# Where to fetch 22 streamed weight granules: spread over the whole segment, or over its q, k, v projections alone

## The chip, the cores and the metric

The kernel runs on one core of a Trainium2 chip. The metric is the device time of one execution in microseconds (us), as the median of several runs. The word "clock" means the mean granted TensorE clock as a share of full speed.

## The reference, cut to what matters

The work is a layer norm, a recurrent attention with memory (A), and a small expert part at the end (B). Part A is nearly all of the time:

```python
mem = mem0                                        # 8 rows
for s in range(64):                               # 64 segments of 32 rows, width 1024
    h = concatenate([mem, x[s]])                  # 40 rows
    q, k, v = h @ Wq, h @ Wk, h @ Wv              # each to 32 heads x 128
    p = softmax(where(mask, q @ k.T * scale, -1e9))
    o = (p @ v) @ Wo                              # the output projection
    mem = o[:8]                                   # goes into the next segment
    outs.append(o[8:])
```

The four weight matrices are 8 MB each in bf16, and every segment needs all 32 MB. Neither kernel keeps them all in the core's memory (42 of 64 pieces stay there, as told below), and a segment can't start before the memory rows of the one before are there.

## The kernel before

The weights are cut into 64 **granules** of 512 KB: 48 for q, k, v (six phases of eight), then 16 for the output projection. 42 are resident; 22 are **streamed**, which means that they are fetched again in each segment into a ring of six slots. Half of each of three of them (`HELD`) stays in PSUM and is copied from there by ScalarE.

```python
N_RES = 42
N_SLOT = 6
HELD = (18, 27, 36)
PHASES = [(0, 0), (1, 0), (0, 1), (1, 1), (2, 0), (2, 1)]   # (0 q, 1 k, 2 v; half)
streamed = set(((2 * i + 1) * NG) // (2 * n_str) for i in range(n_str))   # NG = 64, n_str = 22
# = 1 4 7 10 13 16 18 21 24 27 30 33 36 39 42 45 | 48 50 53 56 59 62: six in the projection
```

A slot is given back, and the next granule is issued on SyncE's queue, when the last matmul that reads the slot is over:

```python
def used(g):
    if g in streamed:
        fetch()          # takes a slot of the ring and issues the next granule's DMA
```

In a segment, 32 rows go through every granule as the main pass (24 new rows and 8 memory rows; `PSm`, then `WO` in the projection). The other 8 rows of each segment do not depend on the memory. They are called the **left rows**, and those of four segments are taken together (`PSl`, `WL`). With j = s % 4, the left rows' pass through q is made at j = 2, through k at j = 3, through v at j = 0, and their output projection at j = 3. The end of a segment reads, cut:

```python
for w in range(16):
    Gv = granule(48 + w)
    project(WO, w, Gv, lhs_main, w == 15)
    if j == 3:
        if 48 + w in streamed:
            project(WL, w, Gv, lhs_left, first=not started)   # 6 passes here
        else:
            deferred.append((w, Gv))
    used(48 + w)
OB = ...                                    # copy of WO by ScalarE and VectorE
for w, Gv in deferred[:3]:
    project(WL, w, Gv, lhs_left)            # 3 passes while the copies run
mem_to_st(OB, nxt["st"])                    # transposes of the memory rows: next segment's operand
# the other 7 left passes follow in the next segment's q and k
OL = one.tile([P, 256], BF16, tag="pm", name="OL")   # output of the left rows; PM of softmax has this tag too
```

## Time and profile before

| | before |
|---|---|
| median of 3 runs | 2130.74 us (2130.5 to 2137.17) |
| profiled run | span 2125.5 us, clock 0.954 |
| TensorE busy | 82% |
| DMA | 768.74 MB, 362 GB/s |
| a segment | 30.9 us: j = 0 to 3 take 31.2, 30.7, 30.9, 30.8 |
| of it the projection | 7.3, 8.9, 9.3, 10.6 us |

The segments' times are worked out from TensorE's rows: from the first main pass of one segment to that of the next, means over the segments of one j. One wait, VectorE's for a store (engine, tile, what it waited for, us in total, times, longest):

```profile
DVE PM L497 <- DMA out_dram<-OL: 59.8, 15, 4.6
```

Softmax's PM shares its buffer with OL, so once in four segments it waits until the store of OL has landed.

### The profile page before, as it was taken

The numbers are of one execution on the slowest core, as the hardware profiler recorded it, in microseconds if no ns is written. First come the engines' busy times: TensorE is split into PE (matmuls) and PEld (weight loads), VectorE is DVE, ScalarE is ACT, GpSimd is POOL, SyncE is SP. The second block draws the span as 40 slices with busy tenths as digits, with TensorE's granted clock in tenths as the row PEclk, the third lists the DMA queues.
The fourth block names the chain that finished last, engine by engine and source line by source line (L and its number), as shares of the span: only waits on it lengthen the run. The fifth ranks groups of instructions, "written<-read, shape, count | busy, mean of one in ns | idle before, by whom it ended". The sixth has DMA issues, their size and how long they took to land.

```text
span 2125.5 us, 82723 instructions
## 1 busy us (share of the span) xinstructions
PE 1732.3 (82%) x36202; PEld 883.3 (42%) x36202; DVE 746.4 (35%) x2328; ACT 713.0 (34%) x1738; POOL 540.6 (25%) x1030
## 2 busy tenths in 40 slices
PE   2678888888889888887888888888888888888776
PEld 1234444444444444444444434444444444444341
DVE  5523332333333233333333333333333333333330
ACT  3533333333333333332333333333333323333220
POOL 4422223222222322222232222223222222222110
PEclk8689999999999999999999999999999999999996
DMA  9899999999999999999999999999999999999998
GB/s 357 333 366 389 337 375 361 381 353 364 377 353 369 361 379 347 360 381 356 371 346 389 348 365 365 372 367 347 372 356 383 358 370 363 347 365 351 350 339 341
DMA packets 294351, 768.74 MB, mean 362 GB/s; under 512 B 37458, under 2 KB 42770, under 8 KB 293988
## 3 DMA queue, kind: packets, MB, share of 16 engines
q1 hardware_dynamic: 267652, 732.79, 93.3%
q0 software_dynamic: 23520, 26.06, 3.7%
q8 instruction: 283, 4.64, 0.8%
q10 hardware_dynamic: 2816, 4.59, 0.6%
q14 instruction: 80, 0.66, 0.1%
HBM read 750.68 MB, written 12.59 MB: 359 GB/s over the span
## 4 chain that ended last, share of the span: by engine, by line
DMA 50%; PE 41%; DVE 3%; issue 3%; ACT 3%; POOL 0%; ACTq 0%; DVEq 0%; SPq 0%; POOLq 0%
DMA g<-in_A_Wo_dram 21%; PE PSm L590 21%; DMA g<-in_A_Wv_dram 11%; DMA g<-in_A_Wq_dram 7%; PE PSl L603 6%; PE OA L641 4%; DMA out_dram<-OL 4%; DMA g<-in_A_Wk_dram 2%; PE WL L641 2%; PE PTq L430 2%; DMA wres<-in_A_Wo_dram 1%; DMA g<-in_B_w_up_dram 1%; PE SPS L474 1%; DMA g<-in_B_w_gate_dram 1%; PE PTq L442 1%
## 5 line engine op out<-in xcount | busy, mean ns | idle before, releaser
L590 PE MATMUL PSm<-wres,ST 128*32 128x512 bf16 x8192 | 757.0, 394 | 19.7 <-DVE ST L309 17.9
L590 PE MATMUL PSm<-g,ST 128*32 128x512 bf16 x4096 | 415.8, 395 | 98.4 <-DMA g<-in_A_Wv_dram 53.1
L590 PEld LDWEIGHTS <-ST 128*32 128x32 bf16 x12288 | 294.3, 97 | 429.8 <-issue 198.8
L641 PEld LDWEIGHTS <-OT 128*32 128x32 bf16 x8192 | 215.8, 98 | 170.8 <-issue 156.4
L220 ACT COPY g<-HELD 128x1024 bf16<-128x1024 bf16 x189 | 191.3, 1012 | 204.6 <-PE PSm L590 115.4
L611 ACT CAST XB<-PSm 128x512 bf16<-128x512 f32 x256 | 150.2, 587 | 322.2 <-PE PSm L590 321.6
L641 PE MATMUL OA<-wres,OT 128*32 128x256 bf16 x5120 | 236.1, 280 | 18.8 <-issue 12.7
L641 PE MATMUL OA<-g,OT 128*32 128x256 bf16 x3072 | 160.2, 280 | 95.9 <-DMA g<-in_A_Wo_dram 89.4
L603 PE MATMUL PSl<-wres,STL 128*32 128x512 bf16 x2048 | 199.9, 391 | 14.0 <-DVE XBl L615 13.4
L340 POOL DMA_DIRECT2D QKL<-qkl_d x126 | 92.1, 731 | 264.3 <-issue 118.3
L538 ACT CAST OT<-OA 128x128 bf16<-128x128 f32 x256 | 68.2, 266 | 267.8 <-PE OP L532 266.0
L462 POOL COPY KT<-QKL 128x128 bf16<-128x128 bf16 x128 | 37.8, 295 | 415.9 <-PE OA L641 310.1
L676 POOL DMA_DIRECT2D out_dram<-OB x256 | 129.8, 514 | 52.3 <-DVE OB L672 35.9
L538 DVE CAST OT<-OP 128x128 bf16<-128x128 f32 x128 | 37.3, 292 | 265.1 <-PE OP L532 265.1
L603 PEld LDWEIGHTS <-STL 128*32 128x32 bf16 x3072 | 86.0, 99 | 97.8 <-issue 38.4
L479 DVE TENSOR_REDUCE NM<-SPS 128x8 f32<-128x320 f32 x128 | 62.9, 491 | 158.3 <-PE SPS L474 158.3
L623 ACT CAST VM<-PSm 128x512 bf16<-128x512 f32 x128 | 77.2, 603 | 120.1 <-PE PSm L590 114.9
L603 PE MATMUL PSl<-g,STL 128*32 128x512 bf16 x1024 | 103.0, 392 | 11.5 <-DVE XBl L615 8.7
L430 PE MATMUL PTq<-IDENT,XB 128*128 128x128 bf16 x1024 | 103.7, 225 | 5.5 <-ACT XB L611 5.0
L450 POOL DMA_DIRECT2D qkl_d<-QS x64 | 36.6, 572 | 278.4 <-ACT QS L446 278.4
L430 PEld LDWEIGHTS <-XB 128*128 128x128 bf16 x1024 | 59.3, 99 | 114.6 <-ACT XB L611 60.6
L437 DVE COPY KT<-PTq 128x512 bf16<-128x512 bf16 x128 | 53.4, 417 | 134.8 <-PE PTq L430 134.5
(140 smaller groups left out, 2310.3 us busy)
## 6 DMA issues: line engine op xcount, KB each, us to landing
g<-in_A_Wo_dram SPq DMA_DIRECT2D x384, 512.0 KB, 7.2
g<-in_A_Wq_dram SPq DMA_DIRECT2D x321, 512.0 KB, 7.6
g<-in_A_Wk_dram SPq DMA_DIRECT2D x257, 512.0 KB, 6.5
g<-in_A_Wv_dram SPq DMA_DIRECT2D x257, 512.0 KB, 7.2
g<-in_A_Wq_dram SPq DMA_DIRECT2D x63, 256.0 KB, 5.9
g<-in_A_Wk_dram SPq DMA_DIRECT2D x63, 256.0 KB, 5.5
g<-in_A_Wv_dram SPq DMA_DIRECT2D x63, 256.0 KB, 7.0
qkl_d<-QS POOLq DMA_DIRECT2D x64, 128.0 KB, 6.1
```

Of the source, the lines that this page charges most:

```text
L220: nc.scalar.copy(out=t[:, 1024:2048], in_=held[what[1]][:, :].bitcast(BF16))
L340: nc.gpsimd.dma_start(out=t[:, :, :], in_=qkl_d[s // 4][:, half, :, s % 4, :].rearrange("m p c -> p m c"))
L430: nc.tensor.transpose(out=PTq[:, il, :, :].rearrange("p j r -> p (j r)"), in_=XB[:, il * P:(il + 1) * P], identity=IDENT[:, :])
L437: nc.vector.tensor_copy(out=keys(half)[:, :, 0:32], in_=pv)
L479: nc.vector.tensor_reduce(out=NM[:, :], in_=S8, axis=AX.X, op=ALU.max, negate=True)
L538: copy(out=OT[half][:, 2 * ph + jl, :, :], in_=ov[:, :, 0:SEG])
L590: nc.tensor.matmul(PSm[32 * jq:32 * jq + 32, :], lhsT=ST[:, kc, :], rhs=Gv[:, 512 * jq:512 * (jq + 1)], start=(kc == 0), stop=(kc == KC - ...
L603: nc.tensor.matmul(PSl[32 * jq:32 * jq + 32, :], lhsT=cur["stl"][:, kl, :], rhs=Gl[:, 512 * jq:512 * (jq + 1)], start=(kl == 0), stop=(kl ...
L611: nc.scalar.copy(out=XB[:, :], in_=PSm[:, :])
L623: nc.scalar.copy(out=VM[half][:, :], in_=PSm[:, :])
L641: nc.tensor.matmul(PS[32 * g:32 * g + 32, 0:256], lhsT=lhs(h), rhs=Gv[:, D * hs + 256 * g:D * hs + 256 * (g + 1)], start=(first and hs == ...
L676: nc.gpsimd.dma_start(out=out2[s * SEG:s * SEG + XM, 256 * g:256 * (g + 1)], in_=OB[32 * g:32 * g + XM, 0:256])
```

## The change

It makes the whole output projection resident and spreads the 22 streamed granules over the 48 of q, k, v. The intent is that the projection waits for no transfer, and that the DMA, which ran below its best rate in the middle of q, k, v, gets more to do there. Left rows' passes become filler: at j = 1 and 2 the next segment's left passes of q or k on resident granules are put around the transposes of the memory rows, and at j = 3 all 16 left projection passes are made in the projection and around the transposes. OL moves to another buffer. Cut to its core:

```diff
-HELD = (18, 27, 36)
+HELD = (14, 22, 29)
-    streamed = set(((2 * i + 1) * NG) // (2 * n_str) for i in range(n_str))
+    streamed = set(((2 * i + 1) * 48) // (2 * n_str) for i in range(n_str))
+    # = 1 3 5 7 9 12 14 16 18 20 22 25 27 29 31 33 36 38 40 42 44 46
 ...
-            project(WO, w, Gv, lhs_main, w == 15)
+            project(WO, w, res_tiles[48 + w], lhs_main, w == 15)
+            if j == 3:
+                if w == 2:
+                    XLT = load_left(G, again=True)      # was at w == 8
+                if 5 <= w < 14:
+                    project_left()                      # 9 passes here
 ...
-        for w, Gv in deferred[:3]:
-            project(WL, w, Gv, lhs_left)
+        if j == 3:
+            fill = [project_left] * (16 - n_wl)
+        elif j == 1 or j == 2:
+            for mat in nl:                              # next segment's left passes of q or k
+                begun[mat] = left_bank()
+                fill = [lambda ...: left_pass(L, kc, res_tiles[g])
+                        for kc in range(KC) if 8 * mat + kc not in streamed]
+        for fn in fill[:len(fill) // 2]:
+            fn()
         if s + 1 < NSEG:
             mem_to_st(OB, nxt["st"])
+        for fn in fill[len(fill) // 2:]:
+            fn()
 ...
-                OL = one.tile([P, 256], BF16, tag="pm", name="OL")
+                OL = one.tile([P, 512], BF16, tag="vm", name="OL")
```

More of the change, by code (lines that the diff above doesn't have):

```diff
@@ L72 @@
     n_str = NG - N_RES
-    streamed = set(((2 * i + 1) * NG) // (2 * n_str) for i in range(n_str))
+    streamed = set(((2 * i + 1) * 48) // (2 * n_str) for i in range(n_str))
+    N_LATE = 10
     assert all(g in streamed and g < 48 for g in HELD)
@@ L208, in fetch @@
                 pool = wres
-                if g >= 48:
+                if g >= NG - N_LATE:
                     if late["pool"] is None:
@@ L390, in routed_e, with left_of, left_pass, left_bank @@
         nc.vector.tensor_copy(out=SIG[:, :], in_=PSG[0:2, 0:1])
+    def left_of(s):
+        G, j = divmod(s, 4)
+        if s == 0:
+            return {0: 0, 1: 0, 2: 0}
+        if j == 0:
+            return {2: G}
+        return {j - 2: G + 1} if j >= 2 and G + 1 < NT else {}
+    def left_pass(L, kc, Gv):
+        for jq in range(4):
+            nc.tensor.matmul(L["ps"][32 * jq:32 * jq + 32, :], lhsT=cur["stl"][:, kc, :],
+                             rhs=Gv[:, 512 * jq:512 * (jq + 1)], start=(not L["had"]), stop=(len(L["had"]) == KC - 1),
+                             tile_position=(0, 32 * jq))
+        L["had"].append(kc)
+    def left_bank():
+        return {"ps": psL.tile([P, 512], F32, tag="accl", name="PSl"), "had": []}
+    begun = {}
     for s in range(NSEG):
         G, j = divmod(s, 4)
-        if s == 0:
-            left = {0: 0, 1: 0, 2: 0}
-        elif j == 0:
-            left = {2: G}
-        elif j >= 2 and G + 1 < NT:
-            left = {j - 2: G + 1}
-        else:
-            left = {}
+        left = left_of(s)
         VM = {}
@@ L582 @@
             PSm = psA.tile([P, 512], F32, tag="acc", name="PSm")
-            PSl = psL.tile([P, 512], F32, tag="accl", name="PSl") if mat in left else None
+            L = begun.pop(p, None) or left_bank() if mat in left else None
             lag, behind = 2 if j == 0 else 0, []
@@ L595 @@
                                             op0=ALU.bitwise_or)
-                if PSl is None:
+                if L is None:
                     used(g)
@@ L601 @@
                     kl, Gl = behind.pop(0)
-                    for jq in range(4):
-                        nc.tensor.matmul(PSl[32 * jq:32 * jq + 32, :], lhsT=cur["stl"][:, kl, :],
-                                         rhs=Gl[:, 512 * jq:512 * (jq + 1)], start=(kl == 0), stop=(kl == KC - 1),
-                                         tile_position=(0, 32 * jq))
+                    if kl not in L["had"]:
+                        left_pass(L, kl, Gl)
                     used(8 * p + kl)
@@ L612 @@
                 hooks.setdefault((p + 1, (3, 2, 3, 2)[p]), []).insert(0, lambda m=mat, h=half, b=XB: transposes(m, h, b))
-                if PSl is not None:
+                if L is not None:
                     XBl = two.tile([P, 512], BF16, tag="xb", name="XBl")
-                    (nc.scalar.copy if p == 2 else nc.vector.tensor_copy)(out=XBl[:, :], in_=PSl[:, :])
+                    (nc.scalar.copy if p == 2 else nc.vector.tensor_copy)(out=XBl[:, :], in_=L["ps"][:, :])
                     hooks.setdefault((p + 1, (5, 4, 6, 4)[p]), []).insert(
@@ L619 @@
                 c0 = half * 512
-                if PSl is not None:
-                    nc.scalar.copy(out=VL[:, c0:c0 + 512], in_=PSl[:, :])
+                if L is not None:
+                    nc.scalar.copy(out=VL[:, c0:c0 + 512], in_=L["ps"][:, :])
                 VM[half] = one.tile([P, 512], BF16, tag="vm", name="VM")
@@ L649, in lhs_left, with project_left @@
             return OTL[:, h, :, :].rearrange("p s r -> p (s r)")
-        deferred = []
-        started = False
+        n_wl = 0
+        def project_left(WL=WL if j == 3 else None):
+            nonlocal n_wl
+            project(WL, n_wl, res_tiles[48 + n_wl], lhs_left, first=(n_wl == 0))
+            n_wl += 1
         for w in range(16):
@@ L657 @@
                 attend(1, 1)
-                if j == 3:
+            project(WO, w, res_tiles[48 + w], lhs_main, w == 15)
+            if j == 3:
+                if w == 2:
                     XLT = load_left(G, again=True)
-            Gv = granule(48 + w)
-            project(WO, w, Gv, lhs_main, w == 15)
-            if j == 3:
-                if 48 + w in streamed:
-                    project(WL, w, Gv, lhs_left, first=not started)
-                    started = True
-                else:
-                    deferred.append((w, Gv))
-            used(48 + w)
+                if 5 <= w < 14:
+                    project_left()
         OB = one.tile([P, 512], BF16, tag="vm", name="OB")
@@ L679 @@
         todo = [((0, 2), store)]
-        for w, Gv in deferred[:3]:
-            project(WL, w, Gv, lhs_left)
+        fill = []
+        nl = left_of(s + 1) if s + 1 < NSEG else {}
+        if j == 3:
[3 more added lines that the diff above has]
+                begun[mat] = left_bank()
+                fill = [lambda kc=kc, g=8 * mat + kc, L=begun[mat]: left_pass(L, kc, res_tiles[g])
+                        for kc in range(KC) if 8 * mat + kc not in streamed]
+        for fn in fill[:len(fill) // 2]:
+            fn()
         if s + 1 < NSEG:
             mem_to_st(OB, nxt["st"])
+        for fn in fill[len(fill) // 2:]:
+            fn()
         if j == 3:
-            spots = [(0, 1), (0, 3), (0, 5), (0, 7), (1, 1), (1, 3), (1, 5), (1, 7), (2, 1), (2, 3)]
-            for pk, (w, Gv) in zip(spots, deferred[3:]):
-                todo.append((pk, lambda w=w, Gv=Gv, WL=WL, lhs=lhs_left: project(WL, w, Gv, lhs)))
             def left_norm(G=G, X=XLT):
@@ L693, in left_store @@
                 residual(WL, X[:, 0:256], P, False)
-                OL = one.tile([P, 256], BF16, tag="pm", name="OL")
-                nc.scalar.copy(out=OL[:, :], in_=WL[:, 0:256])
+                OL = one.tile([P, 512], BF16, tag="vm", name="OL")
+                nc.scalar.copy(out=OL[:, 0:256], in_=WL[:, 0:256])
                 o4 = out2[4 * G * SEG:4 * (G + 1) * SEG, :].rearrange("(s r) d -> s r d", s=4)
                 for g in range(4):
-                    nc.gpsimd.dma_start(out=o4[:, XM:SEG, 256 * g:256 * (g + 1)], in_=OL[32 * g:32 * (g + 1), :])
+                    nc.gpsimd.dma_start(out=o4[:, XM:SEG, 256 * g:256 * (g + 1)], in_=OL[32 * g:32 * (g + 1), 0:256])
             todo += [((0, 6), left_norm), ((1, 6), left_store)]
```

## The prediction

> **What bounds the kernel now.** A segment is one round of q, k, v (48 weight granules of 512 KB), attention, and the output projection (16 granules). 42 granules stay in the chip; 22 are fetched again in each of the 64 segments through six slots, three of them by half. I read the page first, then the DMA share and rate by stretch, then who waited for whom, then the instructions at a segment's end.
>
> From the page, the engines' busy time, the DMA total and the chain that ended last:
>
> ```profile
> PE 1732.3 (82%) x36202; PEld 883.3 (42%) x36202; DVE 746.4 (35%) x2328; ACT 713.0 (34%) x1738; POOL 540.6 (25%) x1030
> ...
> DMA packets 294351, 768.74 MB, mean 362 GB/s; under 512 B 37458, under 2 KB 42770, under 8 KB 293988
> ...
> DMA 50%; PE 41%; DVE 3%; issue 3%; ACT 3%; POOL 0%; ACTq 0%; DVEq 0%; SPq 0%; POOLq 0%
> ```
>
> Half of the chain is transfers, 41% is TensorE, so the bound must change hands inside a segment. Stretches of two segments show it (columns: window, length, busy time of PE, PEld, DVE, ACT, POOL, granted clock, DMA share, GB/s):
>
> ```profile
> 1009.20:1013.00 3.80, 3.80 (x69) 1.71 (x69) 0.78 (x4) 1.13 (x2) 2.11 (x5) 1.00 1.02 409
> 1013.00:1019.00 6.00, 6.00 (x102) 2.69 (x98) 1.80 (x4) 3.66 (x5) 0.85 (x2) 1.00 0.98 332
> 1019.00:1026.00 7.00, 6.76 (x162) 3.25 (x154) 3.78 (x11) 2.48 (x5) 1.69 (x4) 1.00 0.98 347
> 1029.40:1039.90 10.50, 6.04 (x166) 4.08 (x165) 1.26 (x7) 1.70 (x8) 1.11 (x3) 1.00 1.04 410
> 1039.90:1053.00 13.10, 13.10 (x240) 6.11 (x244) 4.91 (x14) 5.80 (x8) 3.35 (x8) 1.00 0.97 337
> ```
>
> In the output projection (1029.4 to 1039.9) TensorE works 6.0 of 10.5 us and the DMA runs at 410 GB/s: transfers bind. In the middle of q, k, v TensorE has no gap and the rate is 332 to 347: the slots are full and TensorE binds. The DMA share says 0.97 in both, so I go by the rate. The waits agree (engine, line, waited for, us in total, times, longest):
>
> ```profile
> PE OA L641 <- DMA g<-in_A_Wo_dram: 89.4, 147, 2.5
> PE PSm L590 <- DMA g<-in_A_Wv_dram: 53.1, 81, 2.6
> PE PSm L590 <- DMA g<-in_A_Wq_dram: 23.0, 38, 2.1
> PE PSl L603 <- DVE XBl L615: 22.1, 3, 8.7
> PE PTm L308 <- ACT OB L671: 20.3, 48, 0.4
> PE PSm L590 <- DMA g<-in_A_Wk_dram: 19.6, 32, 2.3
> PE PSm L590 <- DVE ST L309: 17.9, 63, 0.3
> ```
>
> TensorE waits 185 us for streamed weights (89.4 + 53.1 + 23.0 + 19.6), 2.9 us a segment. A segment takes 30.9 us: the copies that end a segment (OB) run from 115.4 to 2063.8, 63 segments. The end of one:
>
> ```profile
> 1007.43 0.40 PE L641 MATMUL OA<-wres,OT 128*32 128x256 bf16 x8
> 1008.26 0.23 PE L308 MATMUL PTm<-IDENT,OB 128*128 128x128 bf16 x1 [0.42 <-ACT OB L671]
> 1008.65 0.23 PE L308 MATMUL PTm<-IDENT,OB 128*128 128x128 bf16 x1 [0.17 <-DVE OB L672]
> 1009.16 0.40 PE L590 MATMUL PSm<-wres,ST 128*32 128x512 bf16 x4 [0.28 <-DVE ST L309]
> 1009.39 0.39 PE L603 MATMUL PSl<-wres,STL 128*32 128x512 bf16 x4
> ```
>
> 0.42 + 0.17 + 0.28 = 0.87 us of idle TensorE around the memory rows' transposes, and 0.22 us from one pass to the next.
>
> **What the Trainium skill says.** Perfetto Trace Analysis, Optimization Strategy: where the most contended engine changes over time, interleaving the regimes may help. The trace has two such regimes; before, the streamed granules are already interleaved with both, and the change separates them. DMA: Bandwidth & Descriptors, "Anatomy of one DMA", gives about 2.0 us fixed cost for a DMA, mostly the receipt (for GpSimd's path). Here granules go through SyncE: the shortest issue-to-landing time of a 512 KB granule in the trace is 3.39 us, for one issued 7.7 us after the granule before it, and 1.3 us of that is data at 410 GB/s, so about 2.1 us fixed: it agrees. The same page, "Where 436 GB/s comes from", sets about 358 GB/s for HBM to SBUF and 435 for the fabric. The trace sustains 410, and 428 in one stretch of 2 us (1054 to 1056), so 358 doesn't bind and I take 415.
>
> **The change, part by part.** Bytes do not change: still 22 granules, three by half, 10.75 MB a segment; with the other traffic (queues 0 and 8, 30.7 MB over 64 segments) 11.23 MB, or 27.1 us at 415 GB/s: 1.32 us a whole granule (11.23 MB over 20.5 granules), 0.66 a half one. Now all 22 sit between granules 1 and 46 of q, k, v.
>
> (a) TensorE's own time. Summing its rows by the segment's place in a group of four (j = 0 to 3) and taking out the DMA waits, I get 29.1, 25.8, 27.3, 29.4 us, mean 27.9. No matmul is added or removed. Filler hides at most 0.87 us in three segments of four, so the mean falls to some 27.5. That can't be had while transfers need 27.1 plus idle time.
>
> (b) The gap without a release. After granule 46 no slot comes free until granule 1 of the next segment is used. From the start of granule 46 to the residual's matmul is 1.14 us (1028.29 to 1029.43). From there to the next segment's first pass, DMA waits taken out, the trace has 6.6 (j = 0), 7.1, 7.1 and 9.6 us. The change moves work into it: for j = 1 four left passes (granules 0, 2, 4, 6; 0.87 us, mostly hidden, so about 6.9 in all, from j = 0's base), for j = 2 five (7.1), for j = 3 all 16 left projection passes instead of 9, 7 more by 0.22, less the hidden waits and some DMA waits not recognised as such: 9.4. In j = 0 the lagging left passes of v add 0.65. Two more passes and the release, 0.7 us, end it. Gap: 6.6 + 0.65 + 1.85 = 9.1, then 8.75, 8.95, 11.25; mean 9.5 us.
>
> (c) What the DMA can do in the gap: refill six slots, 6 x 1.32 = 7.9 us. Then it idles, and it starts again with one granule, number 14, a half one: 3.4 - 0.65 = 2.75 us until it lands.
>
> (d) The cycle from granule 46 to the next granule 46: gap 9.5, restart 2.75, then the other 15 streamed granules, 13 x 1.32 + 2 x 0.66 = 18.5. Sum 30.75 us, against 30.9 before. TensorE needs about 27.5 for it, so it waits for transfers in the second half of q, k, v instead of in the projection.
>
> So the 89 us of Wo waits go, and Wv, Wk and Wq waits grow by about as much. Over 63 segments 0.15 us are 9 us.
>
> (e) Start and end. The first segment loads the same 64 granules; the last ten still need the prologue's memory back. The last segment fills six slots for the expert's weights during the projection, as before. I take 0 for both, with 5 us of doubt.
>
> (f) A side change: the tile OL moves from tag "pm" to "vm". VectorE waited 59.8 us in 15 waits with PM for OL's store to land. That goes, but ScalarE will wait with OL for OB's stores, issued about 12 granules earlier. Both lie in j = 0's q, k, v, where TensorE would now wait for weights anyway: 0 to 1 us each, 10 us in all at most.
>
> Sum: 2130.7 - 9, and a few us for (f): 2120.
>
> **Rivals.** First, smoothing works: six full slots at the start of q, k and no wait in the projection let TensorE run near its own 27.5 us. Half of the way there is 29.2, 107 us less, 2024. For it speak the 89.4 us of Wo waits in the chain and that the starved DMA of q, k, v gets work. Against it: 27.1 us of transfers must then fit with almost no idle time, and the gap makes idle time in each segment. Second, the gap costs more: the restart ramps slowly, and the left passes added to the projection stand where nothing is released. One us more a cycle gives 2183. The 9.4 us of j = 3 speak for it: that cycle alone comes to 32.5. Third, the swap comes out even, as reckoned. A fourth, that the new OL wait stalls ScalarE and thereby the transposes of k, would show in j = 0 only, at 2 to 3 us by 16: up to 40 us.
>
> **Range and chances.** The sum hangs on two small differences, so 0.8 us a segment of doubt, some 50 us, is fair, with more room downward than upward, since an error in the gap or in the restart can go only as far as TensorE's bound. Range 2055 to 2185. Beyond 2% either way needs 43 us, 0.68 us a segment. Faster 0.33, within 2% 0.46, slower 0.21.
>
> **What would show it.** Right: no wait of OA for a Wo granule; waits of PSm for Wv, Wk and Wq together near 200 us; a rate over 400 GB/s in v; in the last 2 us or more of the projection, and longest for j = 3, a rate well under 200; first landings 3 us after granule 1. Wrong: if segments of j = 3 are no longer than others, the gap isn't the cost; if the rate in the projection stays at 400 to its end, the slots were not refilled and (c) falls; if waits for streamed weights fall below 100 us, the first rival holds.

## The result, and the profile after

| | before | after |
|---|---|---|
| median of 4 runs | 2131.62 us | 2386.43 us (2380.71 to 2395.69) |
| profiled run | 2125.5 us, clock 0.954 | 2379.1 us, clock 0.909 |
| segment, j = 0 to 3 | 31.2, 30.7, 30.9, 30.8 us | 33.7, 33.0, 34.8, 37.9 us (mean 34.9) |
| of it the projection | 7.3, 8.9, 9.3, 10.6 us | 6.9, 7.1, 7.6, 10.6 us |

The kernel got slower by 12%: the ratio is 1.1194, with a 95% interval from 1.1148 to 1.1239.

From the page after, the totals and the chain that ended last:

```profile
PE 1834.6 (77%) x36202; PEld 931.2 (39%) x36202; DVE 749.1 (31%) x2328; ACT 714.8 (30%) x1738; POOL 541.7 (23%) x1030
...
DMA packets 245967, 768.74 MB, mean 323 GB/s; under 512 B 37458, under 2 KB 42770, under 8 KB 245604
...
DMA 55%; PE 37%; issue 3%; ACT 2%; DVE 2%; POOL 0%; ACTq 0%; DVEq 0%; SPq 0%; POOLq 0%
```

The same matmuls and the same bytes took longer. TensorE's busy time rose by 102 us with the same number of matmuls. The lower clock accounts for most of it: 1732.3 us at a clock of 0.954 would be 1818 at 0.909, 86 us more (an estimate). The DMA's mean rate fell from 362 to 323 GB/s, and the chain has more of transfers in it.

TensorE's waits after (who waited for what, us in total, times, longest), and one of ScalarE's:

```profile
PE PSm L605 <- DMA g<-in_A_Wv_dram: 176.9, 278, 2.6
PE PSm L605 <- DMA g<-in_A_Wq_dram: 155.1, 164, 3.3
PE PSm L605 <- DMA g<-in_A_Wk_dram: 37.1, 68, 1.8
PE PTm L309 <- ACT OB L685: 7.2, 17, 0.4
```

```profile
ACT XB L624 <- DMA out_dram<-OL: 55.0, 14, 5.2
```

No streamed Wo granule is left to wait for, as intended. But the waits for Wv, Wq and Wk are 369 us (176.9 + 155.1 + 37.1), against 95.7 before and about 200 predicted. The transposes (PTm) wait for OB 17 times, once in each segment with j = 0, instead of 48 times.

The end of a segment with j = 2 and the start of the next, as TensorE ran it (start, length, line, what, count; a wait stands in brackets):

```profile
1026.25 1.93 PE L654 MATMUL OA<-wres,OT 128*32 128x256 bf16 x64
1028.01 0.60 PE L405 MATMUL PSl<-wres,STL 128*32 128x512 bf16 x8
1028.61 0.56 PE L309 MATMUL PTm<-IDENT,OB 128*128 128x128 bf16 x2
1029.09 0.83 PE L405 MATMUL PSl<-wres,STL 128*32 128x512 bf16 x12
1029.75 0.39 PE L605 MATMUL PSm<-wres,ST 128*32 128x512 bf16 x4
...
1036.76 0.40 PE L605 MATMUL PSm<-g,ST 128*32 128x512 bf16 x4 [1.62 <-DMA g<-in_A_Wq_dram]
```

Between the last projection pass and the first main pass no wait is left: the left passes (PSl) do cover the three waits of 0.42, 0.17 and 0.28 us that stood there before. Seven us into the new segment TensorE waits for a weight.

SyncE's issues of granules around that point, and the same time in stretches (window, length, busy time of PE, PEld, DVE, ACT, POOL, clock, DMA share, GB/s):

```profile
1020.40 1.75 SPq L223 DMA_DIRECT2D g<-in_A_Wk_dram  x2
1030.40 0.33 SPq L220 DMA_DIRECT2D g<-in_A_Wk_dram  x1
1030.83 1.48 SPq L223 DMA_DIRECT2D g<-in_A_Wq_dram  x3
1032.93 0.33 SPq L220 DMA_DIRECT2D g<-in_A_Wq_dram  x1
1034.24 1.09 SPq L223 DMA_DIRECT2D g<-in_A_Wk_dram  x2
```

```profile
1018.00:1027.00 9.00, 7.32 (x184) 4.74 (x187) 2.71 (x10) 2.61 (x14) 0.55 (x1) 0.81 1.01 407
1028.00:1031.00 3.00, 2.90 (x51) 1.14 (x41) 0.48 (x2) 0.86 (x2) 2.12 (x5) 1.00 0.10 33
1031.00:1035.00 4.00, 4.00 (x65) 1.71 (x64) 1.57 (x6) 2.02 (x3) 0.84 (x2) 1.00 0.78 197
1035.00:1044.00 9.00, 6.70 (x109) 2.84 (x104) 2.11 (x4) 3.19 (x5) 0.97 (x3) 0.81 1.03 397
```

The last issue before the pause ends at 1022.15; the next comes at 1030.40. The six slots are filled meanwhile, at 407 GB/s, and then the DMA stands still (33 GB/s from 1028 to 1031). That is the gap as predicted. What was not predicted comes next: from 1031 to 1035 four granules have been issued within 2 us, then more, and the rate is only 197 GB/s. In the 9 us after 1035 TensorE works 6.7 us, and the DMA is at 397. The DMA share says 0.78 at 197 GB/s. The Trainium skill, Perfetto Trace Analysis, "Identifying the Most-Contended Engine", says that the occupancy of the 16 DMA engines misleads; this trace agrees.

Averaged over segments, from the first issue after the pause on, the rate in one us after another is 33, 218, 186, 230, 289, 359, 360, 349, 390, and then about 405 for some us. Individual packets of 4096 B mostly take 159 ns. Of those that start 1 to 4 us after the first issue, 28% take 300 ns or more (mean of all 297 ns); at 10 to 14 us it is 1% (mean 164 ns).

### The profile page after: what moved, and what is told of

The parts are those of the page before. It is cut to its first block, busy times and chain, and to the rows that moved or that the text cites. A ratio compares the mean times of both kernels' runs of the same rounds, so it can differ in the third digit from the quotient of the medians.

```text
span 2379.1 us, 82768 instructions
## 1 busy us (share of the span) xinstructions
PE 1834.6 (77%) x36202; PEld 931.2 (39%) x36202; DVE 749.1 (31%) x2328; ACT 714.8 (30%) x1738; POOL 541.7 (23%) x1030
## 4 chain that ended last, share of the span: by engine, by line
DMA 55%; PE 37%; issue 3%; ACT 2%; DVE 2%; POOL 0%; ACTq 0%; DVEq 0%; SPq 0%; POOLq 0%
DMA g<-in_A_Wv_dram 32%; DMA g<-in_A_Wq_dram 18%; PE PSm L605 14%; PE OA L654 11%; PE PSl L405 4%; PE WL L654 3%; PE OA L545 2%; DMA wres<-in_A_Wo_dram 1%; PE PTq L445 1%; DMA g<-in_B_w_up_dram 1%; PE PTm L309 1%; PE OA L547 1%; DMA g<-in_A_Wk_dram 1%; PE OA L303 1%; DMA XP<-in_A_x_dram 1%
## 5 line engine op out<-in xcount | busy, mean ns | idle before, releaser
L605 PE MATMUL PSm<-g,ST 128*32 128x512 bf16 x5632 | 599.7, 413 | 373.4 <-DMA g<-in_A_Wv_dram 176.9
L605 PE MATMUL PSm<-wres,ST 128*32 128x512 bf16 x6656 | 685.4, 410 | 6.0 <-DVE ST L310 5.1
L605 PEld LDWEIGHTS <-ST 128*32 128x32 bf16 x12288 | 325.7, 97 | 803.9 <-issue 588.5
L654 PE MATMUL OA<-wres,OT 128*32 128x256 bf16 x8192 | 325.8, 294 | 41.1 <-issue 29.1
L654 PEld LDWEIGHTS <-OT 128*32 128x32 bf16 x8192 | 229.7, 103 | 70.3 <-issue 52.6
L405 PE MATMUL PSl<-wres,STL 128*32 128x512 bf16 x1664 | 157.5, 393 | 19.2 <-DVE XBl L628 13.4
L405 PE MATMUL PSl<-g,STL 128*32 128x512 bf16 x1408 | 142.9, 390 | 9.0 <-DVE XBl L628 8.7
L545 PEld LDWEIGHTS <-VM 32*128 32x128 bf16 x2048 | 65.2, 93 | 89.7 <-issue 73.6
```

What stands on the lines that cost most here:

```text
L405: nc.tensor.matmul(L["ps"][32 * jq:32 * jq + 32, :], lhsT=cur["stl"][:, kc, :], rhs=Gv[:, 512 * jq:512 * (jq + 1)], start=(not L["had"]), ...
L545: nc.tensor.matmul(o, lhsT=VM[half][q0:q0 + 32, il * P:(il + 1) * P], rhs=PTm[q0:q0 + 32, il, 0:NK], start=True, stop=False, tile_position ...
L605: nc.tensor.matmul(PSm[32 * jq:32 * jq + 32, :], lhsT=ST[:, kc, :], rhs=Gv[:, 512 * jq:512 * (jq + 1)], start=(kc == 0), stop=(kc == KC - ...
L654: nc.tensor.matmul(PS[32 * g:32 * g + 32, 0:256], lhsT=lhs(h), rhs=Gv[:, D * hs + 256 * g:D * hs + 256 * (g + 1)], start=(first and hs == ...
```

## The experiments

The first theory after the result was: the pause of about nine us in the giving back of slots costs the time, because transfers come back slowly after it (**pause theory**). Its rivals were: the filler and the left passes' new places cost it (**filler theory**); the half granule with which transfers restart (**half granule**); TensorE's lower clock (**clock theory**); and, later, that the q, k stage with its main passes slows transfers whatever came before (**stage theory**), or that the queue is short because the slots come free one by one (**supply theory**). Fourteen runs were made (none has the number 7); all results were correct.

### e1_place: the new placement alone

The changed kernel's placement and OL, with the left rows' work as before: no early passes, the left projection 6 + 3 + 7.

```diff
-                if 5 <= w < 14:
-                    project_left()
+                if w in (0, 2, 5, 8, 11, 14):
+                    project_left(w, Gv)
 ...
-        # filler around mem_to_st at j = 1, 2, 3
+        for _ in range(3 if j == 3 else 0):
+            project_left(*pend.pop(0))       # before mem_to_st; the other 7 in the next q, k
```

> The new placement of the streamed granules alone; the left rows' passes and the left projection stand where they stood before (6 of the 16 left projection passes in the projection, 3 ahead of the transposes, 7 in the next q and k; no left pass begun early). Pause theory (no slot comes free during the projection, the transfers stop, and come back slowly): the pause stays, only shorter by about 1.5 us for j = 3 and 0.3 us for j = 1 and 2, so 16 x (1.5 + 0.6) = 34 us off: about 2350, 2310 to 2385. Filler theory (the left passes moved into the projection are what costs): near before, 2100 to 2160.

It took 2357.54 us, ratio 1.1064 (1.1011 to 1.1116), clock 0.913. The placement alone brings nearly all of the loss, so the filler theory falls.

### e2_filler: the new left rows' work alone

The changed kernel with the old placement and HELD; the left passes go around the transposes as in the change, and a left projection pass on a streamed granule stays beside its main pass.

```diff
-HELD = (14, 22, 29)
+HELD = (18, 27, 36)
-    streamed = set(((2 * i + 1) * 48) // (2 * n_str) for i in range(n_str))
+    streamed = set([1, 4, 7, ..., 42, 45, 48, 50, 53, 56, 59, 62])
```

> The filler and the moved left projection alone, with the placement of before (six streamed granules in the projection). Pause theory: slots come free all through the projection, so no stop of the transfers; 2080 to 2145, about 2115, since 0.9 us of idle TensorE around the transposes is used in half of the segments. Filler theory: most of the 250 us stays, above 2250.

It took 2105.37 us, ratio 0.9871 (0.983 to 0.9913), clock 0.952: a little faster than before. With e1_place this settles that the placement is the cost and the rest of the change a small gain.

### e3_mix2, e4_mix4, e11_mix8: two, four, eight of the 22 in the projection

They are e2_filler with other lists, and HELD moved to fit. For e11_mix8 the ten last-loaded resident granules are loaded by a step of their own in the first segment.

```diff
+    streamed = set([1, 3, 6, ..., 44, 46, 52, 60])                      # e3_mix2
+    streamed = set([1, 4, 6, ..., 44, 46, 50, 54, 58, 62])              # e4_mix4
+    streamed = set([1, 5, 8, ..., 42, 46, 49, 51, 53, 55, 57, 59, 61, 63])  # e11_mix8
```

> As the changed kernel, but 2 of the 22 streamed granules in the projection (its granules 4 and 12), 20 in q, k, v. Pause theory: the longest stretch without a release falls from 9 us to about 4, less than the six slots hold, so the transfers never stop: 2060 to 2170, and no stretch of a microsecond under 150 GB/s between segments. Filler theory: above 2250 still.

It took 2231.66 us, ratio 1.0487 (1.0425 to 1.0549). The expectation missed: I had thought that two releases in the projection break the pause and so cure it. Transfers do not stop any more, but the mean rate in the us after the start of a segment is still 230, 133, 239, 242, 251, 285, 318 (none under 150 was expected). On average 1.2 granules are under way in the first of these us and 4.1 in the fifth. ("Under way" means issued and not landed; the trace has 16 landing events for each granule, and each is counted as a sixteenth.) So it needs no full stop; a queue run nearly dry is followed by the same low rates.

> As the changed kernel, but 4 of the 22 streamed granules in the projection (2, 6, 10 and 14). Pause theory: no stop, and more of the transfers lie in q, k, v than before, where TensorE has most to do: 2040 to 2130, the best of the four if the old placement had too much in the projection. Filler theory: above 2250.

It took 2133.99 us, ratio 0.9988 (0.9917 to 1.0059), just above the range that I expected.

> As the changed kernel, with 8 of the 22 streamed granules in the projection. With 0, 2, 4 and 6 (placement of before) the times were 2386, 2232, 2134 and 2105. If the releases should keep pace with time and the projection with its attention takes 8.7 of 31 us, 22 x 8.7 / 31 = 6.2 is the best number, and 8 gives TensorE more waits in the projection: 2110 to 2170. If every release moved to the end helps: under 2095.

It took 2233.7 us, ratio 1.0485 (1.0439 to 1.0532), clock 0.890: a miss, in the other direction. Here TensorE waits 168.7 us for Wo granules in the projection. With the six of e2_filler the times over the number of granules in the projection (0, 2, 4, 6, 8) are 2386, 2232, 2134, 2105 and 2234 us. The old place, six, is the best of these.

### e5_held: no half granule at the restart

```diff
-HELD = (14, 22, 29)
+HELD = (20, 29, 38)
```

> As the changed kernel, with other halves held back (granules 20, 29, 38 for 14, 22, 29), so that the first transfer after the pause is a whole granule with 4 KB rows and no copy by ScalarE. If the half granule makes the start slow: the rate in the 2nd to 4th us after the first release rises from about 220 to over 350 GB/s and the time falls by 1 us a segment or more, under 2325. If it is the start after a pause as such: the same 190 to 250 GB/s, and 2386 within 25.

It took 2414.73 us, ratio 1.1326 (1.1251 to 1.1402). The rates in the second to sixth us are 207, 291, 222, 237, 327: as slow as with a half granule first. The half granule is not the cause. The run is even a little slower than the changed kernel (1.1326 against 1.1194, and just outside the range expected); why was not followed up.

### e6_warm: keep TensorE's clock up

Unneeded passes on a resident granule are put before each streamed v granule at j = 1 to 3, where TensorE waits for it anyway.

```diff
+                if mat == 2 and L is None and s > 0 and g in streamed:
+                    for jq in range(4):
+                        nc.tensor.matmul(DUM[...], lhsT=ST[:, kc, :], rhs=res_tiles[32][...], start=True, stop=True, ...)
```

> As the changed kernel, with a pass into an unused bank ahead of each streamed v granule in j = 1 to 3 (0.22 us each, while TensorE would wait anyway), so that TensorE doesn't fall idle at the end of v. Its results are unused. Clock theory (TensorE, idle at the end of v, is granted half the clock in the first 3 us of the projection, which lengthens the pause): the granted clock rises from 0.91 to over 0.94, the projection is about 1 us shorter in three segments of four, 2386 - 48 = 2338 or less. If the clock isn't on the path: 2370 to 2420, whatever the clock does.

It took 2370.67 us, ratio 1.1157 (1.1097 to 1.1218), and the clock rose from 0.909 to 0.934. The Trainium skill, TensorE: Matmul & The Clock Gate, "What's actually happening", says that the clock drops to half after an idle window of about 3.4 us; the traces agree with a clock of 0.50 in stretches after TensorE stood nearly still (e10_pause_v and e15_six below). But getting back more than half of the lost clock (0.025 of 0.045) brought back 16 us of 255, and the intervals of the two kernels overlap. So the lower clock is at most a small part of the cost. That it comes from the waiting is likely, but not shown.

### e8_slot7: a longer queue

Seven slots, 41 resident granules, 23 streamed ones.

```diff
-N_RES = 42
-N_SLOT = 6
-HELD = (14, 22, 29)
+N_RES = 41
+N_SLOT = 7
+HELD = (13, 21, 28)
```

> As the changed kernel, with seven slots and 41 resident granules: 23 streamed, so 1.3 us more of transfers a segment, and a pause 1.3 us shorter. If the cost is the pause alone, both cancel: 2386 within 20. If a fixed cost comes with each time that the transfers have run dry, and seven slots avoid that in j = 0 to 2 (gaps of 7.5 to 8.9 us against 9.2 us of refill): 3 us in three segments of four less, about 2386 - 140 = 2245. If the transfers come back slowly in any case: 2350 to 2450.

It took 2430.19 us, ratio 1.1395 (1.1334 to 1.1457). It has one granule more to fetch, 64 times 0.52 MB, which at 415 GB/s is 81 us, so the time alone does not tell much. The rates do: from the start of a segment on they are 22, 68, 268, 345, 313, 293, 330, 268, 262, 310, 383, 404, while from the third us on three to six granules are under way. One slot more does not cure the slow return.

### e9_burst and e14_six: two void tests of the supply theory

Both were to give back several slots at one time, by calling the fetch for all of them later in the program: e9_burst (from e2_filler) those of the projection at its end, e14_six (from the changed kernel) the first six at granule 12.

```diff
-            used(48 + w)
+            if s == 0 or s > 58:
+                used(48 + w)
 ...
+        for w in range(16 if 0 < s <= 58 else 0):
+            used(48 + w)                          # e9_burst
```

```diff
     def used(g):
-        if g in streamed:
+        if g in streamed and not (0 < s < 60 and g in at_once):
             fetch()
+        if 0 < s < 60 and g == at_once[-1]:
+            for _ in at_once:
+                fetch()                           # e14_six
```

> The placement of before with the filler (2105), but the six slots of the projection are given back all together at the segment's end (segments 1 to 58), so that six transfers are issued at once after a pause. It tells how transfers start. If the slow start comes from slots given back one by one: 380 GB/s or more from the 2nd us after the first issue on. If transfers start slowly by themselves: 190 to 290 GB/s in the 2nd to 4th us, with three or more granules waiting. Time: the pause plus a start with empty slots, some 4 to 6 us a segment, 2350 to 2470.

> As the changed kernel, but in segments 1 to 59 the first six slots of a segment (granules 1, 3, 5, 7, 9, 12) are given back together after granule 12, so that six transfers are issued in one go after the pause, some 3 us later than before. If the slow start comes from transfers that are issued one by one into an empty queue: over 380 GB/s from the 2nd us after the first issue on, and the full start makes up for the 3 us, 2386 within 40. If a pause is followed by a slow start whatever is waiting: 190 to 320 GB/s for 4 us or more again, and 3 us a segment more, about 2570.

They took 2104.98 us (ratio 0.9891, 0.9838 to 0.9945) and 2376.72 us (ratio 1.1165, 1.1084 to 1.1246), the times of the kernels that they were made from. The issue times in the traces had not moved. SyncE's queue holds nothing but these transfers, and each waits only for the last reader of its slot, wherever the call stands in the program of the other engines. Neither run says anything on the theory.

### e10_pause_v: the same pause elsewhere

The pause is moved into v: 16 streamed granules in q and k, none in v, six in the projection (from e2_filler, late loads as in e11_mix8).

```diff
-HELD = (18, 27, 36)
+HELD = (13, 19, 25)
+    streamed = set([1, 3, 5, ..., 29, 31, 54, 56, 58, 60, 62, 63])
```

> The pause moved: 16 streamed granules in q and k (1, 3, ... 31), none in v, six in the projection (its granules 6, 8, 10, 12, 14, 15), so that no slot comes free from the end of k to the middle of the projection, about 9 us. If transfers come back slowly after any pause: full rate at the start of q (over 380 GB/s in the first 4 us), and after the first release in the projection 190 to 320 GB/s for some 5 us or more; the time well over before, 2250 to 2450. If it is the q, k stage that slows transfers, whatever came before: over 380 GB/s within 3 us of the first release in the projection, and 190 to 320 at the start of q.

It took 2365.88 us, ratio 1.1094 (1.1042 to 1.1146). The mean pause between issues is 9.45 us, and after it the rates are 14, 204, 322, 242, 271, 291, 306, 344, 374, 402. From the first issue of q on they are 298, 317, 348, 380, 396, 408; over 380 in the first 4 us was expected, and it is reached only in the fourth. One such cycle in stretches (columns as above); slots come free again at 1144.9, in the projection:

```profile
1136.00:1144.90 8.90, 7.64 (x213) 4.42 (x205) 4.08 (x13) 3.45 (x14) 1.79 (x3) 1.00 0.85 318
1144.90:1149.00 4.10, 4.00 (x114) 2.69 (x110) 0.87 (x4) 0.62 (x3) 0.93 (x3) 1.00 0.63 221
1149.00:1154.00 5.00, 1.40 (x25) 0.59 (x21) 0.46 (x3) 1.01 (x1) 1.36 (x3) 0.93 0.87 303
1154.00:1160.00 6.00, 5.69 (x50) 1.76 (x53) 1.10 (x4) 1.50 (x2) 0.66 (x1) 0.50 1.03 409
```

After the pause the rate is 221, then 303, then 409 GB/s. In the third stretch TensorE works 1.40 of 5 us, and in the fourth its clock is 0.50. The slow return follows the pause into the projection, so the stage theory falls as the main cause. That the start of q slows transfers somewhat (298 to 348 GB/s in its first three us) is not excluded.

### e15_six: six slots truly at one time

After granule 12, six one-column matmuls read the six slots once more. Now they are the last readers, and the slots come free together.

```diff
+                if early and g == at_once[-1]:
+                    for i, Ge in enumerate(early):
+                        nc.tensor.matmul(DUM[0:SEG, i:i + 1], lhsT=ST[:, kc, :], rhs=Ge[:, 0:1], start=True, stop=True, ...)
+                    for _ in at_once:
+                        fetch()
```

> As e14 was meant: the trace of e14 showed its transfers issued as before, since the queue of transfers waits for a slot's last reader alone and not for the place in the program. Here six one-column matmuls after granule 12 read the first six slots once more, so that they really come free together (segments 1 to 59). Slow start because of transfers issued one by one into an empty queue: 380 GB/s or more from the 2nd or 3rd us after the first issue on; 2386 within 45, the full start making up for the delay. A pause is followed by a slow start whatever waits: 190 to 320 GB/s in the 2nd to 5th us after the first issue, and about 3 us a segment more, 2570.

It took 2642.29 us, ratio 1.2379 (1.229 to 1.2467), more than I had expected, with a mean pause of 13.1 us. SyncE's issues and the us after them, one by one:

```profile
1063.10 0.33 SPq L221 DMA_DIRECT2D g<-in_A_Wk_dram  x1
1063.52 1.91 SPq L224 DMA_DIRECT2D g<-in_A_Wq_dram  x3
1065.52 0.71 SPq L221 DMA_DIRECT2D g<-in_A_Wq_dram  x1
1066.32 1.78 SPq L224 DMA_DIRECT2D g<-in_A_Wk_dram  x2
```

```profile
1064.00:1065.00 1.00, 0.00 (x0) 0.00 (x0) 0.00 (x0) 1.00 (x2) 0.24 (x1) 1.00 0.77 248
1065.00:1066.00 1.00, 0.08 (x4) 0.08 (x7) 0.00 (x0) 0.03 (x1) 0.00 (x0) 0.67 0.59 165
1066.00:1067.00 1.00, 0.96 (x8) 0.20 (x8) 0.00 (x0) 0.00 (x0) 0.00 (x0) 0.50 0.76 193
1067.00:1068.00 1.00, 0.00 (x0) 0.00 (x0) 0.00 (x0) 0.59 (x1) 0.00 (x0) 0.50 0.93 328
1068.00:1069.00 1.00, 0.00 (x0) 0.00 (x0) 0.00 (x0) 0.00 (x0) 0.00 (x0) 0.50 1.05 397
```

Four of the six have been issued by 1065.43 and the sixth at 1066.32, 3.2 us after the first. So from two to six granules were in the queue, little else ran, and still the us from 1064 to 1067 bring 248, 165 and 193 GB/s. The first, a half granule, landed 2.77 us after its issue, as predicted for one alone. Over all segments the rates from the first issue on are 6, 258, 183, 216, 261, 373, 393. In these 7 us that is 1.69 MB; in the changed kernel, where the slots come free one by one, it is 1.68 MB. The six issues take 2.7 us on average instead of 3.8, and granules land 2.8, 5.9, 7.3 and 8.7 us after the first issue instead of 3.2, 6.1, 7.5 and 9.1. So giving the slots back together gains next to nothing, and the supply theory falls, as far as this run can test it: SyncE's issues are 0.4 to 0.7 us apart, and a faster supply was not tried.

The run speaks against two more rivals. In the changed kernel TensorE works 4.00 us of the 4 slow us from 1031 to 1035. Here it does next to nothing from 1064 to 1066, at similar rates (248 and 165 GB/s against 197), so its work is not what slows the transfers. And the other DMA queues move only 0.5 to 6 GB/s on average in the first six us after the first issue.

### e12_ol: the OL buffer, with the earlier load

The kernel before with OL in its new buffer and the earlier load of XLT.

```diff
-                OL = one.tile([P, 256], BF16, tag="pm", name="OL")
+                OL = one.tile([P, 512], BF16, tag="vm", name="OL")
```

> The kernel before with two small parts of the change alone: OL in the other tag, and the left rows' second load six granules earlier. If the 59.8 us that VectorE waited for OL's store were on the path of j = 0: 1 to 2 us in each of 16 segments, 2100 to 2115, and the filler gives nothing of the 25 us that it gained with the old placement. If they were off it: 2131 within 10, and the filler gives all.

It took 2110.01 us, ratio 0.989 (0.985 to 0.993): nearly the whole gain of e2_filler. Which of the two parts gives it was not separated. VectorE's wait of 59.8 us is gone, and segments with j = 0 take 30.39 instead of 31.23 us.

### e13_left: the best version

It is e12_ol with the change's early left passes of q and k around the transposes, and the left projection where it was before.

```diff
+        fill = []
+        for mat in left_of(s + 1) if j in (1, 2) and s + 1 < NSEG else ():
+            begun[mat] = left_bank()
+            fill = [lambda ...: left_pass(L, kc, res_tiles[g]) for kc in range(KC) if 8 * mat + kc not in streamed]
+        for fn in fill[:len(fill) // 2]:
+            fn()
         mem_to_st(OB, nxt["st"])
+        for fn in fill[len(fill) // 2:]:
+            fn()
```

> The kernel before with the OL tag (2110) and the early left passes of q and k around the transposes (j = 1 and 2) alone; the left projection as before. The sum of segments from the runs with and without the filler: j = 1 loses 0.4 us in the projection, j = 2 and 3 gain 0.8 and 0.6 in q, k, v, 16 x 1.0 = 16 us: 2095, 2080 to 2112. If q, k, v is bound by transfers whatever TensorE does: 2110 or slower.

It took 2084.31 us, ratio 0.9793 (0.9747 to 0.9839): faster than both kernels, though the interval does not settle whether by more than 2%. Against e2_filler it lacks only the moved left projection passes. The two intervals barely overlap, which speaks for these passes costing some of the gain; I have no direct comparison.

## Why the prediction was wrong, point by point

**(a) TensorE's own time and the filler.** "Filler hides at most 0.87 us in three segments of four" held: the waits around the transposes are gone in three segments of four. On the old placement it is worth about 20 us (e13_left against e12_ol, 0.979 against 0.989). On the new one the left rows' new places cost some 28 us instead (1.1194 against 1.1064 in e1_place): the pause at the end of j = 3 is 12.0 us, against 10.5 in e1_place. TensorE's time was never the bound of the changed kernel.

**(b) The gap** was right in the mean. With no issue there are 7.5, 8.8, 8.9 and 12.0 us at j = 0 to 3, mean 9.3. Predicted were 9.1, 8.75, 8.95 and 11.25, mean 9.5, counted from the start of granule 46, which is some 0.44 us earlier. So j = 0 was put 1.2 us too long and j = 3 1.2 us too short; that the two cancel is luck. The j = 3 segments are the longest, as said.

**(c) and (d) failed**, at "it starts again with one granule ... 2.75 us until it lands, then the other 15 streamed granules, 13 x 1.32 + 2 x 0.66 = 18.5". The first landing was nearly as reckoned (3.15 us on average, and 2.77 us for the one shown of e15_six), but the 1.32 us a granule was the full rate taken from a queue that never runs dry. From the first issue after the pause until granule 46 is released it takes 25.6 us. The prediction's terms make 21.7 of this (2.75 + 18.5 + 0.44), so 3.9 us are missing. With the pause, which is 0.2 us longer than predicted, the cycle takes 4.1 us more than the 30.75. Over 63 cycles that is 258 us; the time missed the predicted 2120 by 266.

What of the 3.9 us can be worked out: in the first 9 us 2.41 MB move (the sum of the rates above). With data from 0.9 us on at 415 GB/s it would be 3.36 MB, so 2.3 us are lost. The landing events show where: the first four granules land 3.15, 6.06, 7.53 and 9.10 us after the first issue, and the prediction's terms give 2.75, 4.07, 5.39 and 6.71. The second granule, issued 0.5 us after the first, lands 2.9 us after it instead of 1.32, and from the fourth on little is added. In the 16.5 us after the first 9 the rate is 393 instead of 415, which loses 0.9 us. About 0.7 us I can't place. That the slow return after the pause is what costs is shown by e1_place (placement alone), e10_pause_v (pause elsewhere, the same return) and e15_six. The second rival, "the restart ramps slowly", was the right mechanism; I gave it one us a cycle, a quarter of what it is.

The profile before held a hint, which I misread. I took its 332 to 347 GB/s in q, k as slots being full, and wrote that the DMA share was 0.97 in both stages; it was 1.04 in the projection and 0.97 to 0.98 in q, k, v. Worked out from the landing events, 3.6 to 4.3 granules were under way between 9 and 13 us after a segment's start, where the rate was 282 to 306 GB/s, and 3.4 to 3.9 in the first 7 us, at 363 to 398. So transfers that had been issued ran below their best rate in that kernel too, without a pause. Why is not shown.

**The waits** of PSm for weights were to be near 200 us and were 369, for the same reason. "No wait of OA for a Wo granule", "a rate well under 200" at the projection's end and about 400 GB/s afterwards all held: they test the gap, not the restart.

**(e)** was not tested on its own. The first segment takes 4.5 us more than before (99.8 against 95.2), with 11.7 us of waits for resident Wo granules; that is within the 5 us of doubt.

**(f)** had the right wait and the wrong worth: "10 us in all at most" for the OL buffer. On the old placement, together with the earlier load of XLT, it gave 1.1%, some 23 us (e12_ol). In the changed kernel ScalarE did get a wait for OL's store, 55.0 us in 14 waits, but at the XB copy and not with OL for OB's stores; in e12_ol the same wait is 1.3 us. Why it differs I did not follow up.

**What stays open** is why transfers run at half rate after a pause. Many packets themselves take longer, and the DMA engines stand idle for a part of the time (share 0.78 from 1031 to 1035); that is all the traces show.

## What to carry to other kernels

Place streamed loads so that slots keep coming free in every stage of a loop, the stage with spare transfer time included: a pause in the releases costs its own length beyond what the slots can hold, and then a restart that brought about half the rate for some four us here. When working out a cycle with a pause, don't take the sustained rate for the time after it; look in the trace for a place where the queue has just run dry and take the rate from there. And try each part of a combined change alone: the buffer of one small tile (with an earlier load) and the filler, here worth 2% together, were buried under a placement that cost 11%.

## What the Trainium skill lacked or had wrong

- DMA: Bandwidth & Descriptors, "Anatomy of one DMA", gives a fixed cost and a cost per byte. It lacks that the rate itself drops after a pause: 183 to 261 GB/s for four us after a mean pause of 13.1 us though six slots were given back at once (e15_six), and 186 to 289 GB/s when they come one by one after 9 us (the changed kernel). A fixed cost and a full rate would land the second granule 4.07 us after the first issue; it landed after 6.06.
- The same page, "Where 436 GB/s comes from", says that for transfers between HBM and SBUF the HBM side, about 358 GB/s, binds. That does not hold for one core alone, as the page's own measured table has it: with this one core at work, stretches of 6 to 10 us ran at 407 to 410 GB/s.
- Perfetto Trace Analysis, "Identifying the Most-Contended Engine", warns of DMA occupancy, and rightly; it lacks how far off it is: a share of 0.78 at 197 GB/s and 0.97 at 337.
- No page spells out that a later call to fetch in the program doesn't by itself delay the transfer: in e9_burst and e14_six the issue times did not move, since the queue waits only for its slot's last reader.
